# Making all gate terms of an mLSTM in the first stage of a fused attention and two-MLP kernel

## The chip, the cores and the metric

One core of a Trainium2 chip runs the kernel. The metric is the device time of the whole program in microseconds (us). The engines are TensorE (PE, with its weight loads as PEld), VectorE (DVE), ScalarE (ACT), GpSimd (POOL) and SyncE (SP), whose queue issues every DMA of this kernel.

## The reference

Three blocks follow one another, on 2 batches, 8 heads, 768 steps and a head size of 40 (16 rows of gates, 1536 tokens, width 320).

```
# 1: mLSTM, per batch and head, over steps t
m_new  = max(f[t] + m, i[t])
f_stab = exp(f[t] + m - m_new);  i_stab = exp(i[t] - m_new);  m = m_new
C = f_stab * C + i_stab * outer(v[t], k[t]);  n = f_stab * n + i_stab * k[t]
y[t] = sigmoid(o[t]) * (C @ q[t]) / max(abs(n . q[t]), 1)
# 2: x = y (1536 x 320);  h = x @ w_in (2048);  g = piecewise quadratic of h;  x = g @ w_out
# 3: 8 experts of 1024: out = sum_e P[:, e] * (relu(x @ w1[e]) @ w2[e])
#    P: exp of x @ w_gate, normalized eight times over rows and columns
```

## The kernel before, in words

The steps are cut into 6 chunks of L = 128; a chunk of one batch is a tile, so there are 12 tiles t = 0 to 11 (chunk t // 2, batch t % 2), each of 128 tokens and 8 heads.

**Gates.** All gate rows lie in one tile `g_all` (`g_i`, `g_f`, `g_x`, `g_m`). `gate_logs(a, b)` runs the max-plus scan on DVE over columns a to b and then six elementwise steps, on DVE for chunk 0 and on POOL for later columns (L376 to L385). `gate_sums` adds up the logs inside each chunk with a scan on DVE. `store_sums` writes the sums to a DRAM tile `g_d` (four small DMAs), and `load_g(t)` reads them back, spread over 128 partitions (512 KB), as the tile G of a later tile; for tile 0 and 1 `decay` makes G on PE instead. `gate_tokens` (which is `gate_by_token` and `gate_ends`) turns the sums into factors by token with small matmuls and three ACT instructions (`gt`, `nla`, `lend`). Before, chunk 0's gates are made first; chunk 1's follow inside the first stage (logs after `keys(1)`, sums after `gate_out(0)`, `gate_tokens(1, 2)` at its end); chunks 2 to 5 (four chunks, 512 columns) are made by `gates_rest(2, NCH)`, called at the end of tile 2, in the next stage.

**First stage.** Tiles 0 and 1 are written out by hand, with three pieces of the weights of block 2 between them (`pieces`; a piece is loaded raw, decoded by ACT and three DVE steps, and split in two). While `ordered[0]` is true, PE, ACT and DVE each keep the order of the text. SP's queue is in the order of the text too in this trace: `load_g(2)` stands behind `store_sums(1, 2)`.

**Next stage.** After `ordered[0] = False` the planner may reorder. Block 2's loop takes tokens 0 to 511 first, in halves of 256 (`STAGES[0]`): for two tiles of `ff` at tokens 0 to 255 (tiles 0 and 1), with six steps of the generator `attn_rest` after each, then tokens 256 to 511, for which tiles 2 and 3 must be done: until then the loop only pulls steps of `attn`. A tile's `attn` runs `values`, the causal cut of G, eight `Exp` (one a head), `scores`, `gated`, `values_sum`, `update`, `gate_out`, `turn` and `tile_x`, which writes the tile's columns of XH (ACT) and XL (DVE), the inputs of block 2's first product. In `attn(3)`, `sigmoids(4, NTILE)` stands right after `values_sum`; it needs `load_o(4, NTILE)` (1280 KB), issued in `attn(2)`. From the third block on the loop is nothing but matrix products with weights prepared a step ahead.

`warm(n)` issues n matmuls on zeros, which no result uses.

Of the kernel before, what the change touches and what calls it, by code (L numbers as in the profile page):

```python
# [11 lines left out]
ACTF = mybir.ActivationFunctionType  # L12
# [3 lines left out]
B, H, S, D = 2, 8, 768, 40  # L16
# [15 lines left out]


W0 = 14
WD = 3
WA, WG = 4, 2
RATE = (3.1, 4.5, 0, 0, 0)

# [6 lines left out]
def mlstm_moe_moe_kernel(  # L45
# [103 lines left out]
    with ExitStack() as atx:  # L149
# [11 lines left out]
        def load_gates(a, b):  # L161
            for r in range(2):
                nc.sync.dma_start((g_f, g_i)[r][0:GROW, a:b], gates[1 - r, :, a:b])
            nc.sync.dma_start(g_x[96:GROW, a:b], gates[0, 96:GROW, a:b])
# [4 lines left out]
        def store_sums(c0, c1):  # L169
            for j in range(4):  # L170
                o = j // 2 * 8 + j % 2
                nc.sync.dma_start(g_d[j * 4 : j * 4 + 4, (c0 - 1) * L : (c1 - 1) * L], g_x[o : o + 7 : 2, c0 * L : c1 * L])

        def gate_tokens(c0, c1):
            gate_by_token(c0, c1)
            gate_ends(c0, c1)

        def gates_rest(c0, c1):
            gate_logs(c0 * L, c1 * L)
            gate_sums(c0, c1)  # L180
            store_sums(c0, c1)
            gate_tokens(c0, c1)

        def tile_g(t):
            if t in (1, 3):
                return wide[:, t - 1 + t // 3, :].rearrange("p (h t) -> p h t", h=8)
# [6 lines left out]
        def load_qk(t):  # L193
            for r in range(2):
                nc.sync.dma_start(
                    QK[t % 2][r * 64 : r * 64 + 40, 0 : 2 + r : 1 + r], qk[t, r].rearrange("p (a b c) -> p a b c", a=2, b=4)
                )

        def load_kv(t):
            b = ap.tile([128, 648], F32, name="kv_t", tag="kv_t", bufs=2)  # L200
            nc.sync.dma_start(b, kvo[t][:, 0:648])
            return QK[t % 2], b, tile_g(t)

        def load_o(t0, t1):
            nc.sync.dma_start(sig[:, t0:t1, :], kvo[t0:t1, :, 648:968].rearrange("t p d -> p t d"))
# [105 lines left out]
        def load_piece():  # L311
            if len(raws) < len(M1SEQ):
                raws.append(m1_load(*M1SEQ[len(raws)]))

        load_qk(0)
        load_piece()
        load_qk(1)
        load_gates(L, 2 * L)
        tiles_in[0] = load_kv(0)
        tiles_in[1] = load_kv(1)  # L320
        load_piece()
        load_o(0, 2)
        load_piece()
        load_o(2, 4)
        load_piece()

        def m1_weights():
# [40 lines left out]
        def gate_logs(a, b):  # L368

            sl, nx = slice(a, b), slice(a + 1, b + 1)  # L370
            vec.tensor_tensor_scan(
                out=g_m[0:GROW, nx], data0=g_f[0:GROW, sl], data1=g_i[0:GROW, sl], initial=g_m[0:GROW, a : a + 1],
                op0=ALU.add, op1=ALU.max,
            )
            eng = gp if a else vec
            eng.tensor_tensor(out=g_x[0:96, sl], in0=g_f[0:96, sl], in1=g_m[0:96, sl], op=ALU.add)  # L376
            eng.tensor_tensor(out=g_x[0:GROW, sl], in0=g_x[0:GROW, sl], in1=g_m[0:GROW, nx], op=ALU.subtract)  # L377
            q = g_f[0:LROW, sl]
            eng.tensor_scalar(out=q, in0=g_x[0:LROW, sl], scalar1=CLAMP, scalar2=ROUND, op0=ALU.max, op1=ALU.add)  # L379
            eng.tensor_scalar(out=q, in0=q, scalar1=ROUND, scalar2=None, op0=ALU.subtract)  # L380
            q = g_f[64:LROW, sl]
            x = g_x[64:LROW, sl]
            if a:
                gp.tensor_scalar(out=x, in0=x, scalar1=CLAMP, scalar2=None, op0=ALU.max)  # L384
                gp.tensor_tensor(out=q, in0=x, in1=q, op=ALU.subtract)  # L385
            else:
                vec.scalar_tensor_tensor(out=q, in0=x, scalar=CLAMP, in1=q, op0=ALU.max, op1=ALU.subtract)

        def gate_sums(c0, c1):

            for c in range(c0, c1):
                cs = slice(c * L, (c + 1) * L)
                vec.tensor_tensor_scan(
                    out=g_x[0:LROW, cs], data0=ones[0:LROW, :], data1=g_f[0:LROW, cs], initial=0.0, op0=ALU.mult, op1=ALU.add,
                )
            if c0 == 0:
                act(out=gl, in_=g_x[0:48, 0:L], func=ACTF.Copy)
                vec.tensor_tensor(out=gl[32:48], in0=g_x[32:48, 0:L], in1=f(gl[32:48]), op=ALU.subtract)
# [43 lines left out]
        def scores(t, hf, tag):  # L442
            p = bank(tag)
            a = tiles_in[t][0]
            for i in range(4):
                mm(p[:, i * 128 : (i + 1) * 128], a[0:104, 1 + hf, i, :], a[0:104, 0, i, :], start=True, stop=True)
            return p
# [87 lines left out]
        def attn(t):  # L535
            c, b = divmod(t, 2)
            last = c == NCH - 1
            qk_t, _, G = tiles_in[t]
            vw = values(t)
            gp.affine_select(  # L540
                out=G, in_=G, pattern=[[0, 8], [1, 128]], compare_op=ALU.is_ge, fill=FAR, base=0, channel_multiplier=-1,
            )
            for j in range(8):
                h = b * 8 + j % 4 * 2 + j // 4
                act(out=G[:, j, :], in_=G[:, j, :], func=ACTF.Exp, bias=nla[:, c, h : h + 1])
            yield
            if t == 2:
                load_o(4, NTILE)
            A = []
            for hf in range(2):  # L550
                p = scores(t, hf, "at")
                yield
                A.append(gated(t, hf, p))
                yield
            kw = None if last else keys(t)
            pi = bank("ax")
            for pr in range(4):
                mm(pi[:, pr * 82 : (pr + 1) * 82], qk_t[0:104, 0, pr, :], Cst[:, b, pr, :], start=True, stop=True)
            pa = values_sum(A, vw, "at", WA if t < 5 else 0)
            if t == 3:  # L560
                sigmoids(4, NTILE)
            yield
            if not last:
                pu = update(kw, vw, "at")
                gp.tensor_tensor(
                    out=Cst[:, b, :, :], in0=Cst[:, b, :, :],
                    in1=lend[:, c * 8 + b * 4 : c * 8 + b * 4 + 4].unsqueeze(2).to_broadcast([104, 4, 82]), op=ALU.mult,
                )
            hv = ap.tile([128, 8, 41], F32, name="hv", tag="hv")
            vec.tensor_tensor(  # L570
                out=hv, in0=heads(pi), in1=gt[:, c, b * 8 : b * 8 + 8].unsqueeze(2).to_broadcast([128, 8, 41]), op=ALU.mult,
            )
            vec.tensor_tensor(out=hv, in0=hv, in1=heads(pa), op=ALU.add)
            sg = gate_out(t, hv)
            yield
            if not last:
                add_update(t, pu)
            px = turn(sg, "ax")
            yield
            tile_x(t, px)  # L580
            if t == 2:
                gates_rest(2, NCH)
            if t + 2 < NTILE:
                load_tile(t + 2)
            yield
# [16 lines left out]

        gate_logs(0, L)
        gate_sums(0, 1)
        vw, kw, A, pa, pu, px, sg = ({} for _ in range(7))
        pieces = [m1_piece(*M1SEQ[n], raws[n]) for n in range(3)]
        ps_ = {}
# [7 lines left out]
        A[0] = [gated(0, hf, ps_[0, hf]) for hf in range(2)]  # L615
        kw[0] = keys(0)
        next(pieces[0], None)
        decay(1, 0, "g1")
        decay(1, 1, "g1")
        vw[1] = values(1)  # L620
        for hf in range(2):
            ps_[1, hf] = scores(1, hf, "g2")
        A[1] = [gated(1, hf, ps_[1, hf]) for hf in range(2)]
        kw[1] = keys(1)
        gate_logs(L, 2 * L)
        pa[0] = values_sum(A[0], vw[0], "at", 0)
        next(pieces[1])
        sigmoids(0, 2)
        pa[1] = values_sum(A[1], vw[1], "g2", 0)
        pu[0] = update(kw[0], vw[0], "at")  # L630
        sg[0] = gate_out(0, heads(pa[0]))
        gate_sums(1, 2)
        next(pieces[1], None)
        px[0] = turn(sg[0], "ax")
        add_update(0, pu[0])
        store_sums(1, 2)
        load_qk(2)
        tiles_in[2] = load_kv(2)
        load_g(2)
        sg[1] = gate_out(1, heads(pa[1]))  # L640
        pu[1] = update(kw[1], vw[1], "g2")
        next(pieces[2])
        tile_x(0, px[0])
        warm(WD, wbank)
        px[1] = turn(sg[1], "g2")
        add_update(1, pu[1])
        sigmoids(2, 4)
        tile_x(1, px[1])
        next(pieces[2], None)
        warm(WD, wbank)  # L650
        raws[0:3] = [None] * 3
        gate_tokens(1, 2)
        load_piece()
        load_tile(3)
        load_gates(2 * L, S)
        ordered[0] = False
        wjobs = m1_weights()
        w_state = [2]

# [343 lines left out]
```

## Time and profile before

| | before |
|---|---|
| three runs, us | 1003.9, 1005.05, 1005.0 (median 1005.0) |
| the profiled execution, us | 1004.18, of which its span is 1002.4 |
| PE busy | 975.7 us (97%), mean granted clock 0.981 |
| DVE, ACT, POOL busy | 443.9, 373.0, 51.6 us |
| DMA | 52.55 MB, nearly all on SP's queue |

Times in the rows are us from the start of the span. A row of a timeline gives start, length, engine, operation, the tile written and the tile read, the shapes, how many instructions are merged into it, and in brackets the idle time before it with what ended it. A busy PE is not PE at its peak: at a granted clock of 0.50 the same matmul takes about twice as long.

### The profile page before, as it was taken

How to read it: one execution, taken by the hardware profiler on the slowest of the kernel's cores; microseconds unless marked ns; L12 is line 12 of the kernel's file. 1: busy time of each engine (PE TensorE's matmuls, PEld its weight loads, DVE VectorE, ACT ScalarE, POOL GpSimd, SP SyncE). 2: the span in 40 equal slices, each digit the busy share in tenths (PEclk: the TensorE clock that was granted, in tenths of full speed). 3: DMA queues.
4: the chain of work that ended last, by engine and by line, in shares of the span. 5: the costliest groups of instructions: out<-in, count | busy, mean ns of one | idle time of the engine just before them, and what ended most of it. 6: DMA issues, size and time to landing. Idle time of an engine off the chain costs nothing.

```text
span 1002.4 us, 13461 instructions
## 1 busy us (share of the span) xinstructions
PE 975.7 (97%) x5465; PEld 866.7 (86%) x5465; DVE 443.9 (44%) x814; ACT 373.0 (37%) x705; POOL 51.6 (5%) x63
## 2 busy tenths in 40 slices
PE   9859999999999999999999999999999999999998
PEld 6748988888887899999999999999999998999997
DVE  6756686675465563422522432252243234222222
ACT  4736575888775223311411321141132113111111
POOL 4242420000000000000000000000000000000000
PEclk9868999999999999999999999999999999999999
DMA  6834640121003000200300120030021002000000
GB/s 188 252 114 130 191 139 4 53 87 58 0 17 100 1 2 29 87 1 1 116 1 1 51 66 1 1 116 1 1 71 46 1 12 77 1 1 1 27 27 27
DMA packets 44574, 52.55 MB, mean 52 GB/s; under 512 B 3536, under 2 KB 37952, under 8 KB 44512
## 3 DMA queue, kind: packets, MB, share of 16 engines
q1 hardware_dynamic: 44512, 51.69, 17.2%
q8 instruction: 43, 0.70, 0.3%
q14 instruction: 19, 0.16, 0.0%
HBM read 49.67 MB, written 2.01 MB: 52 GB/s over the span
## 4 chain that ended last, share of the span: by engine, by line
PE 93%; DVE 3%; POOL 2%; ACT 1%; issue 1%; DMA 0%; DVEq 0%; SPq 0%; POOLq 0%
PE bk_g L69 74%; PE bk_ax L69 11%; PE bk_at L69 8%; DVE sg L69 1%; DVE den L69 0%; DMA qk<-in_qk_dram 0%; POOL g_all L379 0%; DVE Cst L69 0%; ACT scr L69 0%; DVE dv L69 0%; DVE raw L69 0%; POOL g_all L384 0%; POOL g_all L380 0%; DVE A L69 0%; POOL g_all L377 0%
## 5 line engine op out<-in xcount | busy, mean ns | idle before, releaser
L69 PE MATMUL bk_g<-XH,wk 128*128 128x512 f32 (+1 forms) x1240 | 402.7, 390 | 0.6 <-ACT XH L69 0.6
L69 DVE SCALAR_TENSOR_TENSOR lo<-bk_g,hi 128x512 fp32r<-128x512 f32 x192 | 132.7, 691 | 373.1 <-ACT hi L69 372.0
L69 PE MATMUL bk_g<-XL,wk 128*128 128x512 f32 (+1 forms) x744 | 286.2, 385 | 1.1 <-DVE XL L69 1.1
L69 ACT ACTIVATE hi<-bk_g 128x512 fp32r<-128x512 f32 x192 | 115.1, 599 | 454.2 <-PE bk_g L69 453.6
L69 PEld LDWEIGHTS bk_g<-XH,wk 128*128 128x128 f32 x1240 | 233.0, 190 | 43.5 <-ACT XH L69 1.0
L69 PE MATMUL bk_g<-wf,hi 128*128 128x320 f32 x1152 | 256.1, 308 | 0.0
L69 PEld LDWEIGHTS bk_g<-wf,hi 128*128 128x128 f32 x1152 | 199.4, 188 | 12.9
L69 PE MATMUL bk_g<-wf,lo 128*128 128x320 f32 x576 | 177.3, 308 | 0.0
L69 PEld LDWEIGHTS bk_g<-XL,wk 128*128 128x128 f32 x744 | 141.6, 190 | 23.1 <-DVE XL L69 1.4
L69 PEld LDWEIGHTS bk_g<-wf,lo 128*128 128x128 f32 x576 | 108.0, 187 | 0.2 <-DVE lo L69 0.2
L69 PE MATMUL bk_ax<-wf,hi 128*128 128x320 f32 x384 | 87.1, 308 | 0.0
L69 PEld LDWEIGHTS bk_ax<-wf,hi 128*128 128x128 f32 x384 | 64.2, 187 | 0.0
L69 ACT ACTIVATE gs<-gs 128x512 f32<-128x512 f32 x96 | 60.4, 629 | 1.9
L69 PE MATMUL bk_ax<-wf,lo 128*128 128x320 f32 x192 | 58.4, 304 | 0.0
L69 DVE TENSOR_TENSOR wf<-raw,wf 128x640 fp32r<-128x640 f32 (+2 forms) x48 | 35.9, 757 | 19.5 <-ACT wf L69 19.4
L69 DVE TENSOR_TENSOR gs<-bk_g,gs 128x512 f32<-128x512 f32 x41 | 28.3, 690 | 33.1 <-ACT gs L69 33.0
L69 ACT ACTIVATE wf<-raw 128x640 fp32r<-128x640 f32 (+2 forms) x48 | 31.0, 656 | 29.8 <-DMA raw<-in_w_dram 14.7
L69 ACT ACTIVATE wk<-raw 128x512 fp32r<-128x512 f32 (+1 forms) x42 | 26.8, 638 | 35.9 <-DMA raw<-in_w_dram 21.8
L69 ACT ACTIVATE gs<-bk_g 128x512 f32<-128x512 f32 (+1 forms) x50 | 29.7, 594 | 26.5 <-PE bk_g L69 26.0
L69 DVE SCALAR_TENSOR_TENSOR acc<-bk_g,P,acc 128x320 f32<-128x320 f32 x63 | 30.8, 545 | 15.3 <-PE bk_g L69 15.3
L69 DVE TENSOR_TENSOR wk<-raw,wk 128x512 fp32r<-128x512 f32 x40 | 27.5, 689 | 20.5 <-ACT wk L69 20.3
L69 PEld LDWEIGHTS bk_ax<-wf,lo 128*128 128x128 f32 x192 | 36.0, 188 | 0.0
(186 smaller groups left out, 799.3 us busy)
## 6 DMA issues: line engine op xcount, KB each, us to landing
raw<-in_w_dram SPq DMA_DIRECT2D x32, 320.0 KB
raw<-in_w_dram SPq DMA_DIRECT2D x32, 256.0 KB
raw<-in_w_out_dram SPq DMA_DIRECT2D x8, 640.0 KB
raw<-in_w_in_dram SPq DMA_DIRECT2D x8, 512.0 KB
raw<-in_w_dram SPq DMA_DIRECT2D x64, 64.0 KB
kv_t<-in_kvo_dram SPq DMA_DIRECT2D x12, 324.0 KB
qk<-in_qk_dram SPq DMA_DIRECT2D x24, 160.0 KB
G<-g_d SPq DMA_DIRECT2D x5, 512.0 KB
```

Source lines behind the costliest of these rows:

```text
L69: r = fn(*args, **kw)
```

## The change

All gates are made in the first stage. The logs of chunk 1 move ahead of the first `values`, its sums and `gate_tokens(1, 2)` ahead of `gated(1, ...)`; the logs of chunks 2 to 5 stand between the two `gated` of tile 1, their sums and stores at the end of the first stage, and `gate_tokens(2, NCH)` in `attn(2)`, ahead of its `scores`. `gates_rest` is gone. The transfers are reissued: the gates of chunks 1 to 5 come early, the output gates of tiles 2 and 3 and the fourth piece later, and everything that tiles 2 and 3 need stands behind `load_g(2)` and `load_g(3)`, right after the stores of chunk 1's sums. `sigmoids(2, 4)` moves ahead of `tile_x(0)`. WD grows from 3 to 4, and the warm matmuls go to another bank. The eight `Exp` of a tile are kept behind the last ACT instruction of the first stage.

```diff
-WD = 3
+WD = 4
...
-        def gates_rest(c0, c1):
-            gate_logs(c0 * L, c1 * L)
-            gate_sums(c0, c1)
-            store_sums(c0, c1)
-            gate_tokens(c0, c1)
...
         load_qk(0)
+        load_gates(L, 2 * L)
         load_piece()
         load_qk(1)
-        load_gates(L, 2 * L)
         tiles_in[0] = load_kv(0)
+        load_gates(2 * L, S)
         tiles_in[1] = load_kv(1)
         load_piece()
         load_o(0, 2)
-        load_piece()
-        load_o(2, 4)
         load_piece()
...
-                act(out=G[:, j, :], in_=G[:, j, :], func=ACTF.Exp, bias=nla[:, c, h : h + 1])
+                with tc.issue_after(start_end["act"]):
+                    act(out=G[:, j, :], in_=G[:, j, :], func=ACTF.Exp, bias=nla[:, c, h : h + 1])
             yield
             if t == 2:
+                gate_tokens(2, NCH)
                 load_o(4, NTILE)
...
             tile_x(t, px)
-            if t == 2:
-                gates_rest(2, NCH)
...
         gate_logs(0, L)
         gate_sums(0, 1)
+        gate_logs(L, 2 * L)
...
         next(pieces[0], None)
+        gate_sums(1, 2)
+        store_sums(1, 2)
         decay(1, 0, "g1")
         decay(1, 1, "g1")
         vw[1] = values(1)
-        for hf in range(2):
-            ps_[1, hf] = scores(1, hf, "g2")
-        A[1] = [gated(1, hf, ps_[1, hf]) for hf in range(2)]
+        ps_[1, 0] = scores(1, 0, "g2")
+        ps_[1, 1] = scores(1, 1, "g2")
+        gate_tokens(1, 2)
+        A[1] = [gated(1, 0, ps_[1, 0])]
+        gate_logs(2 * L, S)
+        A[1].append(gated(1, 1, ps_[1, 1]))
         kw[1] = keys(1)
-        gate_logs(L, 2 * L)
+        load_g(2)
+        load_g(3)
+        load_o(2, 4)
+        load_piece()
+        load_qk(2)
+        tiles_in[2] = load_kv(2)
+        load_piece()
+        load_qk(3)
+        tiles_in[3] = load_kv(3)
         pa[0] = values_sum(A[0], vw[0], "at", 0)
         next(pieces[1])
         sigmoids(0, 2)
         pa[1] = values_sum(A[1], vw[1], "g2", 0)
         pu[0] = update(kw[0], vw[0], "at")
         sg[0] = gate_out(0, heads(pa[0]))
-        gate_sums(1, 2)
         next(pieces[1], None)
         px[0] = turn(sg[0], "ax")
-        add_update(0, pu[0])
-        store_sums(1, 2)
-        load_qk(2)
-        tiles_in[2] = load_kv(2)
-        load_g(2)
+        next(pieces[2])
+        sigmoids(2, 4)
         sg[1] = gate_out(1, heads(pa[1]))
         pu[1] = update(kw[1], vw[1], "g2")
-        next(pieces[2])
+        warm(WD, bank("g1"))
         tile_x(0, px[0])
-        warm(WD, wbank)
+        add_update(0, pu[0])
+        next(pieces[2], None)
         px[1] = turn(sg[1], "g2")
+        warm(WD, bank("g1"))
+        tile_x(1, px[1])
         add_update(1, pu[1])
-        sigmoids(2, 4)
-        tile_x(1, px[1])
-        next(pieces[2], None)
-        warm(WD, wbank)
         raws[0:3] = [None] * 3
-        gate_tokens(1, 2)
-        load_piece()
-        load_tile(3)
-        load_gates(2 * L, S)
+        gate_sums(2, NCH)
         ordered[0] = False
+        start_end = dict(newest)
+        store_sums(2, NCH)
```

## Rows read from the trace of the kernel before

**Rows 1.** The page's forty slices of the span (25.1 us each): PE's granted clock.

```profile
PEclk9868999999999999999999999999999999999999
```

**Rows 2.** Windows: stretch, length, then busy time (instructions) of PE, PEld, DVE, ACT, POOL.

```profile
38.70:53.45 14.75, 14.38 (x113) 12.70 (x112) 14.37 (x26) 10.46 (x27) 7.77 (x8) 1.00 0.78 258
...
53.45:86.20 32.75, 18.68 (x89) 17.18 (x89) 18.41 (x37) 15.18 (x27) 9.58 (x7) 0.58 0.45 122
```

**Rows 3.** Timeline of PE: first product of block 2, tile 3, the late gates.

```profile
32.51 0.78 PE L69 MATMUL bk_g<-XH,wk 128*128 128x256 f32 x1
...
53.10 0.35 PE L69 MATMUL bk_at<-vw,A 128*128 128x41 f32 x2
60.70 1.30 PE L69 MATMUL bk_g<-cst,g_all 112*128 112x48 f32 x5 [7.26 <-DVE g_all L69]
63.97 3.77 PE L69 MATMUL bk_g<-cst,g_all 112*128 112x48 f32 x15 [1.96 <-DVE g_all L69]
```

**Rows 4.** Timeline of POOL: chunk 1's six steps, G of tile 2, chunks 2 to 5.

```profile
17.40 0.55 POOL L376 TENSOR_TENSOR g_all<-g_all 96x128 f32<-96x128 f32 x1 [1.74 <-DVE g_all L69]
...
21.18 0.45 POOL L385 TENSOR_TENSOR g_all<-g_all 16x128 f32<-16x128 f32 x1
...
32.40 1.09 POOL L540 TENSOR_SCALAR_AFFINE_SELECT G<-G 128x1024 f32<-128x1024 f32 x1 [0.50 <-DMA G<-g_d]
...
50.06 1.28 POOL L376 TENSOR_TENSOR g_all<-g_all 96x512 f32<-96x512 f32 x1 [1.62 <-DVE g_all L69]
...
58.94 1.25 POOL L385 TENSOR_TENSOR g_all<-g_all 16x512 f32<-16x512 f32 x1
```

**Rows 5.** Timelines of DVE, PE and ACT: end of tile 3, then of tile 4.

```profile
78.62 0.56 DVE L69 TENSOR_TENSOR XL<-bk_ax,XH 128x384 fp32r<-128x384 f32 x1
...
89.36 1.65 PE L69 MATMUL bk_at<-vw,A 128*128 128x41 f32 x14
...
93.74 0.26 ACT L69 ACTIVATE sg<-sg 128x64 f32<-128x64 f32 x1 [0.27 <-DVE sg L69]
...
97.15 0.55 DVE L69 TENSOR_TENSOR XL<-bk_ax,XH 128x384 fp32r<-128x384 f32 x1
```

**Rows 6.** Timeline of ACT: end of the first stage, tile 2's Exp, late sigmoids.

```profile
20.99 0.62 ACT L69 ACTIVATE Cst<-bk_at 40x164 f32<-40x164 f32 x2
...
24.89 0.74 ACT L69 ACTIVATE sig<-sig 128x640 f32<-128x640 f32 x1
...
29.52 1.28 ACT L69 ACT_TABLE_LOAD   x1
...
40.56 1.27 ACT L69 ACTIVATE G<-G,nla 128x128 f32<-128x128 f32 x4
...
68.02 1.28 ACT L69 ACT_TABLE_LOAD   x1
...
71.67 1.28 ACT L69 ACT_TABLE_LOAD   x1
```

**Rows 7.** Timeline of SP's queue: stores of sums, G of tile 2, late output gates.

```profile
22.11 2.53 SPq L172 DMA_DIRECT2D g_d<-g_all  x4
...
26.75 0.38 SPq L191 DMA_DIRECT2D G<-g_d  x1
...
46.23 0.46 SPq L205 DMA_DIRECT2D sig<-in_kvo_dram  x1
```

**Rows 8.** Windows as in rows 2; the last three: PE's clock, DMA share, GB/s.

```profile
2.25:20.25 18.00, 17.43 (x110) 13.05 (x109) 12.61 (x28) 8.00 (x16) 7.14 (x11) 0.99 0.92 258
...
32.50:86.20 53.70, 39.26 (x238) 35.99 (x236) 33.92 (x64) 27.79 (x58) 18.35 (x15) 0.71 0.61 180
100.00:160.00 60.00, 56.99 (x445) 53.16 (x445) 44.50 (x94) 40.62 (x103) 18.34 (x21) 1.00 0.47 139
```

**Rows 9.** Timeline of DVE: one decode step of a piece at two places.

```profile
24.44 0.69 DVE L69 SCALAR_TENSOR_TENSOR dv<-raw,dv 128x512 int32<-128x512 int32 x1
...
52.01 1.11 DVE L69 SCALAR_TENSOR_TENSOR dv<-raw,dv 128x512 int32<-128x512 int32 x1
```

## The prediction, made before the changed kernel ran

> **What bounds the kernel now.** I read the forty slices first, for the stretches where PE is not at full clock: all lie in the first four slices, the first 100 us; behind them it is granted 0.9 or more throughout [rows 1]. So a change to the first stage is worth what it takes out of PE's lost time there. Next the windows: from 53.45 to 86.20 PE is busy 18.68 of 32.75 us at a mean clock of 0.58, against 14.38 of 14.75 at 1.00 in the stretch ahead of it [rows 2]. Work done at full clock is about 18.68 x 0.58 = 10.8 us, so some 22 us are lost in this one stretch. Then PE's timeline says what it waits for: tile 3's `values_sum` has issued two of its sixteen products when small gate products stand next in PE's queue and wait 7.26 us, then 1.96 us, for DVE's sums [rows 3]. POOL's timeline says why these come late: the six steps for chunks 2 to 5 run from 50.06 to 60.19 [rows 4], one behind the other (0.73 us of another step lies among them). The rest of the loss follows from it: after the wait everything PE does for tile 3 runs at the lower clock level (1.2 GHz), tile 3 ends at 79.18 with its XL [rows 5], and the loop can't go on without it.
>
> **The change, part by part.**
>
> *The late gates leave tile 3's path.* Without them `values_sum(3)` goes on at 53.45. Its last 14 products take 1.65 us at full clock, as tile 4's did [rows 5]: 55.1. In tile 4, 6.7 us passed from there (91.01) to the end of XL (97.70) [rows 5]: 61.8. One thing tile 4 did not have: `sigmoids(4, NTILE)` with two table loads holds ACT for 4.93 us (68.02 to 72.95) [rows 6]. Starting at 53.45 it ends at 58.4; tile 4's first ACT step came 2.73 us after its products [rows 5], which is 57.8 here, so it is 0.6 us late. Tile 3 ends at 62.4 in place of 79.18: **-16.8 us**. Bounds: had the planner filled the wait with nothing and the clock stayed full in what follows, a further 3 us would go (the products from 79 to 84 ran at half clock); if the output gates land late (rivals), less. I take no gain in clock: PE still idles some 5 us while tile 3 ends, and behind the wait of 7.26 us the clock was the lower one [rows 2].
>
> *The gate products themselves.* They took 1.30 + 3.77 us at half clock [rows 3], some 2.5 us at full. They now stand in tile 2's stretch, where PE is busy 14.38 of 14.75 us [rows 2], so nothing hides them: **+2.5 us** (0 if they fall in a wait, 5.1 if at half clock).
>
> *POOL and DVE in the first stage.* POOL's ten us of work for chunks 2 to 5 now start behind tile 1's scan, around 17, and end near 27 to 28; tile 2's `values` and causal cut, at 32.40 before [rows 4], are the next to need POOL, so this is covered, with some 4 us to spare. Chunk 1's six steps (17.40 to 21.63, 4.2 us [rows 4]) move to about 8.5 to 13, in front of `values(0)`, which waited for its transfer until 12 anyhow. `keys(1)` could be queued behind the long steps, until 27; only `update(1)` would wait, and the end of the stage is later than that.
>
> *Transfers and ACT.* This is the part that can lose. The first batch sheds 320 + 640 KB and gains 480 KB of gates; at 258 GB/s [rows 8] it ends near 18.4 rather than 20.25. The stores of chunk 1's sums take SP 2.53 us [rows 7]; they can now start near 14 and are down near 19.5, where `load_g(2)` was issued at 26.75 before [rows 7]. Behind it go G of tile 2, G of tile 3 and the output gates of tiles 2 and 3: 1344 KB, 5.3 us at the same rate, plus up to 2.5 us until the first lands (G of tile 2, issued at 26.75 behind two other loads, was down by 32.40 [rows 4, 7]): 24.8 to 27.3. ACT, in the order of the text, gets to `sigmoids(2, 4)` near 23 and waits for that, 2 to 4 us. Queued behind it on ACT are XH of tile 0, two Cst copies, the rest of the third piece, tile 1's copy and XH, and so PE's turn of tile 1. From `sigmoids(2, 4)` to the table load took 4.63 us before (24.89 to 29.52), and the steps that are new behind it add some 1.9 (two Cst copies are 0.62 [rows 6]): block 2's first product starts at 31.4 to 33.9, before at 32.51 [rows 3]. What is saved at this place is the tail of gate work between that table load and the product. I take **+0.5 us**; bounds -1.1 and, with the next paragraph, +4.3.
>
> DVE runs beside POOL more than before: one decode step took 0.69 us with POOL idle and 1.11 us beside POOL's long steps [rows 9]. Two such steps in each of two pieces are 1.7 us, and the lighter steps around them about as much. The Trainium skill ("GPSIMD Engine Reference", "Specifications") says that GpSimd shares its SBUF interfaces with VectorE and contends with DVE instructions that read two SBUF inputs. The trace agrees (0.69 against 1.11 us); by that rule the first stage would end up to 2.9 us later, which is the upper bound just given; I don't add it whole, since ACT, not DVE, ends the stage.
>
> *Tile 2's Exp.* They ended at 41.83, behind ACT's wait for the first product [rows 6]. G and its factors are now there ahead of the stage's end, and the planner can put them first, some 4 us earlier; PE is nearly full there, so I take **-1.0 us** (0 to -4).
>
> *Weights.* DVE does 33.92 us of work between 32.50 and 86.20 [rows 8]; less some 3 us of scans, 31 are left for about 40 us, 78%. Where DVE was at 44.50 of 60 us (74%), PE lost 3.0 of 60 [rows 8]. **+1.5 us**, from 0 to twice that rate (4).
>
> Two more warm matmuls fall in PE's wait for ACT and cost nothing; without that wait, about half a us.
>
> Sum: -16.8 + 2.5 + 0.5 - 1.0 + 1.5 = -13.3. The profiled execution took 1004.18 us (span 1002.4 and 1.8 around it), which gives 990.9; the median of the runs shown is 0.8 above it. I say **991.0 us**. With every term at its worse end (no Exp gain) the sum is -16.8 + 5.1 + 4.3 + 4 = -3.4, with all at the better end about -25.
>
> **The rivals.**
>
> *Smaller gain, a new wait in tile 3.* `load_o(4, NTILE)` was issued at 46.23 [rows 7], behind four pieces, the last of which waits for a buffer that the fifth piece frees. The fourth piece now lands nearly 10 us later, and the stores of chunks 2 to 5 stand ahead of these loads on SP. If the 1280 KB (5.1 us at 258 GB/s) are issued at 53 rather than 46, `sigmoids(4, NTILE)` starts near 59 and ends at 64, and tile 3's XH stands behind it: 6 us lost, 997. Together with a DVE that is full (4 us), 1000. Against it: the raw buffers of the first three pieces are free early.
>
> *Larger gain.* The clock holds behind tile 3 (3 us), Exp early (4), first stage shorter (1): 983.
>
> *Slower.* POOL takes chunk 1's six steps only behind tile 1's `keys`. Then the sums, which stand in DVE's and ACT's order ahead of `gated(1, ...)`, come at 21 rather than 14; stores, both G, the output gates and with them ACT's whole tail move by 7 us and tile 2's queries, behind 960 KB more, by as much: 998. It decides from a shift of 13.3 us: stores not before 27, that is if the long steps are taken first as well. Against it: the text puts chunk 1 first, and its inputs are there by 8 us.
>
> *The gate work doesn't leave the path.* If the planner puts the late sums' products ahead of tile 2 and these wait for POOL, tile 2 is late by what tile 3 was: near 1004, no change. POOL's end near 28 speaks against it.
>
> **How the numbers follow.** Forecast (986 to 995.5): 0.47. Smaller gain (to 1002): 0.26. Larger gain: 0.15. No change: 0.04; slower: 0.08. A range of 983 to 1000 leaves out about 2 in 10. A measurement of this kernel tells about 0.2%, 2 us. Faster by more: 0.88; within: 0.04; slower: 0.08.
>
> **What would show it.** Right: no PE wait on `g_all` beyond 2 us after the first stage, POOL's 512-column steps over by 28, tile 3's XL near 62, stretch 53 to 86 without the long clock dip. ACT's idle before the second sigmoid shows the price of the transfers. Wrong: a wait of over 10 us for SP's transfers ahead of tile 2 or 3, or block 2's first product later than 37.

## The result and the profile after

The changed kernel takes 995.3 us (median of 4 runs, 994.4 to 996.7) against 1004.45 us for the kernel before in the same session (4 runs, 1002.3 to 1005.05): the ratio is 0.9914, with a 95% interval of 0.9893 to 0.9935, so it is faster by 0.9%. The forecast was 991.0 us in a range of 983 to 1000. The profiled execution took 996.17 us (span 994.4, mean granted clock 0.990). On the chips of the experiments below the kernel before spread from 1003 to 1018 us, its long runs at a lower mean clock (1003.38 us at 0.982, 1018.0 at 0.969), while the changed kernel kept to 993.5 to 997.1, so the ratios there stand further from 1; why it spread was not tried.

The page's granted clock of PE in forty slices, beside [rows 1]: the third slice rises from 6 to 7, the fourth from 8 to 9.

```profile
PEclk9879999999999999999999999999999999999999
```

Windows of the changed kernel (columns as in [rows 2]): the end of the first stage, and the stretch from tile 2's end to 72 us, in which tile 3 ends.

```profile
20.25:34.57 14.32, 10.71 (x49) 8.56 (x50) 12.54 (x21) 9.21 (x18) 11.76 (x9) 0.64 0.80 230
...
53.31:72.00 18.69, 11.84 (x74) 10.80 (x76) 17.19 (x34) 10.87 (x16) 3.41 (x3) 0.74 0.83 254
```

The timeline of PE: the first product of block 2, the gate products, `values_sum(3)`, and `turn` of tile 3.

```profile
21.99 3.63 PE L69 MATMUL bk_g<-vw,scr 128*128 128x41 f32 x16 [2.61 <-POOL vw L429]
...
34.57 0.47 PE L69 MATMUL bk_g<-XH,wk 128*128 128x256 f32 x1
...
36.68 1.88 PE L69 MATMUL bk_g<-cst,g_all 112*128 112x48 f32 x16
...
56.80 1.87 PE L69 MATMUL bk_at<-vw,A 128*128 128x41 f32 x16
58.50 0.94 PE L69 MATMUL bk_at<-vw,kw 128*104 128x82 f32 x8
63.97 0.66 PE L69 MATMUL bk_ax<-cst,sg 128*128 128x128 f32 x2 [4.53 <-DVE sg L69]
66.79 0.47 PE L69 MATMUL bk_ax<-cst,sg 128*128 128x128 f32 x1 [2.17 <-ACT sg L69]
```

The reader is to see three things. No wait for `g_all` of the size of [rows 3] is left: the gate products run in 1.88 us at full clock in tile 2's stretch, and `values_sum(3)` goes through at 56.80. But tile 3 now waits elsewhere: its products end at 59.44, and PE stands idle 4.53 us for DVE's `sg`, then 2.17 us for ACT's. And block 2's first product starts at 34.57, 2.06 us later than before.

POOL's timeline says that the order of the change held: chunk 1's steps first, and those of chunks 2 to 5 over by 29.83, though `values(1)` (vw) got its turn between them only at 21.02, which is PE's 2.61 us at 21.99.

```profile
8.37 0.45 POOL L369 TENSOR_TENSOR g_all<-g_all 96x128 f32<-96x128 f32 x1 [4.97 <-DVE g_all L69]
...
11.35 0.45 POOL L378 TENSOR_TENSOR g_all<-g_all 16x128 f32<-16x128 f32 x1
...
18.63 1.26 POOL L369 TENSOR_TENSOR g_all<-g_all 96x512 f32<-96x512 f32 x1 [1.90 <-DMA g_d<-g_all]
...
21.02 0.92 POOL L429 TENSOR_TENSOR vw<-kv_t,gt 128x328 f32<-128x328 f32 x1
...
28.39 1.44 POOL L378 TENSOR_TENSOR g_all<-g_all 16x512 f32<-16x512 f32 x1
```

Timelines of DVE, then of ACT, then of SP's queue.

```profile
21.38 1.10 DVE L69 SCALAR_TENSOR_TENSOR dv<-raw,dv 128x512 int32<-128x512 int32 x1
...
30.56 1.10 DVE L69 TENSOR_TENSOR dv<-raw,wk 64x512 fp32r<-64x512 f32 x1
31.69 1.47 DVE L69 TENSOR_TENSOR wk<-raw,dv 64x512 fp32r<-64x512 f32 x1
...
60.08 0.81 DVE L69 SCALAR_TENSOR_TENSOR dv<-raw,dv 128x640 int32<-128x640 int32 x1
60.82 0.48 DVE L69 TENSOR_TENSOR hv<-hv,bk_at 128x328 f32<-128x328 f32 x1
...
67.96 0.56 DVE L69 TENSOR_TENSOR XL<-bk_ax,XH 128x384 fp32r<-128x384 f32 x1
```

```profile
26.09 0.72 ACT L69 ACTIVATE sig<-sig 128x640 f32<-128x640 f32 x1
...
31.69 1.27 ACT L69 ACTIVATE wk<-dv 64x512 fp32r<-64x512 f32 x2 [1.57 <-DVE dv L69]
32.97 0.26 ACT L69 ACTIVATE sg<-sg 128x64 f32<-128x64 f32 x1
...
62.07 0.87 ACT L69 ACTIVATE wf<-raw 128x512 fp32r<-128x512 f32 x2 [2.12 <-DVE raw L69]
62.96 1.28 ACT L69 ACT_TABLE_LOAD   x1
64.26 2.34 ACT L69 ACTIVATE sig<-sig 128x2560 f32<-128x2560 f32 x1
66.50 0.24 ACT L69 ACTIVATE sg<-sg 128x64 f32<-128x64 f32 x1
...
106.69 1.57 ACT L69 ACTIVATE G<-G,nla 128x128 f32<-128x128 f32 x5 [3.94 <-POOL G L533]
...
108.64 0.24 ACT L69 ACTIVATE sg<-sg 128x64 f32<-128x64 f32 x1
```

```profile
16.23 2.51 SPq L172 DMA_DIRECT2D g_d<-g_all  x4
19.93 0.38 SPq L199 DMA_DIRECT2D sig<-in_kvo_dram  x1
23.64 0.38 SPq L185 DMA_DIRECT2D G<-g_d  x1
...
50.60 0.46 SPq L199 DMA_DIRECT2D sig<-in_kvo_dram  x1
```

Where the 8.0 us between the two spans (1002.4 and 994.4) come from is read off five moments of the two profiled executions: block 2's first product, the end of its first 16 products, the ends of XL of tiles 2 and 3, and that of tile 9 (154.35 before, 146.34 after). The forecast's +1.5 for the weights was worked out for some 40 us from 32.50 on, so it stands with tile 3.

| stretch, us | before | after | difference | forecast |
|---|---|---|---|---|
| start to first product of block 2 | 32.51 | 34.57 | +2.06 | +0.5 |
| its first 16 products (to 36.48, to 36.84) | 3.97 | 2.27 | -1.70 | 0 |
| to XL of tile 2 (52.08, 53.31) | 15.60 | 16.47 | +0.87 | +1.5 |
| to XL of tile 3 (79.18, 68.52) | 27.10 | 15.21 | -11.89 | -15.3 |
| to XL of tile 9 | 75.17 | 77.82 | +2.65 | 0 |
| to the end | 848.05 | 848.06 | 0.0 | 0 |

The sum is -8.0 where the forecast had -13.3.

### The profile page after: what moved, and what is told of

Its sections match the earlier page's. It is cut to its first block, busy times and chain, and to the rows that moved or that the text cites. A ratio compares the mean times of both kernels' runs of the same rounds, so it can differ in the third digit from the quotient of the medians.

```text
span 994.4 us, 13460 instructions
## 1 busy us (share of the span) xinstructions
PE 971.3 (98%) x5461; PEld 862.1 (87%) x5467; DVE 449.7 (45%) x814; ACT 371.6 (37%) x705; POOL 52.8 (5%) x63
## 4 chain that ended last, share of the span: by engine, by line
PE 90%; DVE 5%; ACT 2%; DMA 2%; issue 1%; SPq 0%; POOL 0%; DVEq 0%; POOLq 0%
PE bk_g L69 73%; PE bk_ax L69 11%; PE bk_at L69 6%; DMA raw<-in_w_in_dram 1%; DVE dv L69 1%; DVE den L69 1%; DVE wf L69 1%; DVE raw L69 0%; DVE sg L69 0%; ACT gs L69 0%; DMA raw<-in_w_dram 0%; DVE wk L69 0%; DVE A L69 0%; DVE hv L69 0%; ACT dv L69 0%
## 5 line engine op out<-in xcount | busy, mean ns | idle before, releaser
L69 PEld LDWEIGHTS bk_g<-wf,hi 128*128 128x128 f32 x1152 | 199.3, 188 | 13.3 <-ACT hi L69 0.4
L69 PE MATMUL bk_g<-wf 128*128 128x256 f32 (+1 forms) x192 | 36.0, 326 | 0.3 <-DVE wf L69 0.2
```

What stands on the lines that cost most here:

```text
L69: r = fn(*args, **kw)
```

## The experiments

All kernels were compared with the kernel before on the same chip, where its medians are 1011 to 1014 us. Because of its spread I compare medians with the changed kernel's own, measured again twice (the marks).

The table has all twelve runs. "To first product", "to XL 3" (from the first product) and "to XL 9" (from there) are read from the profiled execution as above. Three profiled executions of the same changed kernel had the first product at 34.57, 35.49 and 36.10, and the five kernels 6 to 10, whose edits lie behind the first stage, at 32.56 to 34.27. So less than 3.5 us is not read from that column.

| kernel | median us | ratio to before (95%) | to first product | to XL 3 | to XL 9 |
|---|---|---|---|---|---|
| changed, second time | 994.85 | 0.982 (0.978 to 0.985) | 36.10 | 33.82 | 76.54 |
| changed, third time | 995.01 | 0.983 (0.979 to 0.987) | 35.49 | 33.87 | 77.84 |
| 1 gates late, rows early | 1008.22 | 0.998 (0.995 to 1.001) | 43.78 | 36.36 | 77.82 |
| 2 before, only gates early | 1008.0 | 0.999 (0.996 to 1.003) | 37.66 | 41.16 | 74.44 |
| 3 gates and rows late | 1005.42 | 0.994 (0.991 to 0.998) | 30.41 | 47.32 | 74.72 |
| 4 logs on DVE | 997.97 | 0.985 (0.981 to 0.988) | 37.11 | 33.95 | 77.72 |
| 5 rows behind the raw piece | 999.45 | 0.986 (0.983 to 0.990) | 37.02 | 34.28 | 77.74 |
| 6 sigmoids behind XH | 994.34 | 0.983 (0.979 to 0.988) | 33.38 | 31.59 | 77.39 |
| 7 zeros in tile 3 | 994.11 | 0.984 (0.980 to 0.988) | 33.24 | 33.80 | 77.22 |
| 8 pieces held | 991.63 | 0.980 (0.976 to 0.984) | 34.27 | 30.58 | 76.74 |
| 9 as 6 and 7 | 996.54 | 0.985 (0.981 to 0.989) | 32.56 | 31.58 | 80.44 |
| 10 as 6, 7 and 8 | 992.05 | 0.981 (0.977 to 0.984) | 33.39 | 30.67 | 78.31 |

1, 2, 6 and 7 ran on one chip, the others on another. Both marks are of the second, so 1, 2, 6 and 7 have none of their own chip.

**The marks.** The changed kernel, unaltered:

> The changed kernel itself once more, as the mark for the runs on this chip: 0.985 to 0.993 of the kernel before; first product of block 2 near 34.6, tile 3's XL near 68.

> The changed kernel once more, unaltered, as the mark for the three kernels run beside it. Expected: 994 to 997 us, block 2's third tile (XL of tile 3) ending 33.5 to 34 us after that of tile 1.

The times came in as expected, and in the third run the rest did too. In the second the ratio, 0.982, lies below the range expected, as the kernel before was slower there, and the first product came at 36.10, 1.5 us later than expected.

### Is it the gates? (1, 2, 3)

**1.** In the changed kernel the gates of chunks 2 to 5 are made at tile 2's end again; their rows are still loaded early.

```diff
-                gate_tokens(2, NCH)
                 load_o(4, NTILE)
...
             tile_x(t, px)
+            if t == 2:
+                gates_rest(2, NCH)
...
-        gate_logs(2 * L, S)
...
-        gate_sums(2, NCH)
...
-        store_sums(2, NCH)
```

> The changed kernel with one part undone: the gates of chunks 2 to 5 are made at the end of tile 2 again; chunk 1's early gates, the new order of transfers and the early Exp stay. Theory G (the gain is the wait for the late gates, taken out of tile 3): PE waits 5 us or more on the sums again, tile 3's XL ends within 3 us of the kernel before's 79.18, and the time is 1002 to 1009, no better than before. Theory T (the gain comes from transfers and Exp being earlier): most of the gain stays, tile 3's XL ends before 73, time below 999.

It was not the undoing that was meant. With their rows in place the planner took the gates into the first stage by itself, and put the sums into DVE's queue where they had to wait. DVE's and PE's timelines of this kernel:

```profile
29.50 0.42 DVE L69 TENSOR_TENSOR_SCAN g_all<-ones,g_all 80x128 f32<-80x128 f32 x1 [7.00 <-POOL g_all L384]
...
34.10 0.90 PE L69 MATMUL bk_ax<-cst,sg 128*128 128x128 f32 x3 [7.01 <-DVE sg L69]
```

DVE stands still for 7.00 us ahead of a sum, with tile 0's `sg` queued behind it, and PE waits 7.01 us for that; block 2 starts at 43.78, 7.7 us or more later than in any execution of the changed kernel. The time is the one that theory G gave, but for another reason. So what is worth having is not early gates alone: the sums must stand where they wait for nothing, as the change has them, written at the stage's end.

**3.** The same, with the rows loaded late too (`load_gates(2 * L, S)` at the end of the stage):

```diff
-        load_gates(2 * L, S)
...
         raws[0:3] = [None] * 3
+        load_gates(2 * L, S)
```

> Mends the run on late gates, where the planner had pulled the late gates into the first stage by itself because their rows were loaded early. Here these rows too are loaded late, as before the change; chunk 1's early gates, the order of the other transfers and the early Exp stay. Theory G (the gain is the wait for the late gates in tile 3): TensorE waits 5 us or more on the late sums in tile 3 again and tile 3's XL ends at 76 to 84; time 1000 to 1008, against the changed kernel's 995. It can keep a few us, since GpSimd is then idle in the first stage and the first product comes 1 to 4 us earlier than in the changed kernel. Theory T (transfers and Exp): XL of tile 3 before 73, time below 999.

Now the old wait is back in PE's timeline, in three parts, and 1005.42 us stands against 994.85 for the changed kernel of the same chip, 10.6 us (7.7 between the two profiled spans, 1002.4 and 994.7):

```profile
52.81 0.31 PE L69 MATMUL bk_at<-vw,A 128*128 128x41 f32 x2
58.27 1.30 PE L69 MATMUL bk_g<-cst,g_all 112*128 112x48 f32 x5 [5.16 <-DVE g_all L69]
61.33 1.30 PE L69 MATMUL bk_g<-cst,g_all 112*128 112x48 f32 x5 [1.75 <-DVE g_all L69]
63.72 2.53 PE L69 MATMUL bk_g<-cst,g_all 112*128 112x48 f32 x10 [1.09 <-DVE g_all L69]
```

The table's row says more: from the first product to tile 3's end it takes 47.32 us instead of 33.82, that is 13.5 us, but the first product comes at 30.41, and at 32.56 to 36.10 in the eight executions with early gates. So the early gates pay 13.5 us and cost the first stage 2 to 6 us. Whether the rest of the change (chunk 1 first, the transfers, the warm products) by itself makes the first stage shorter than before (30.41 against 32.51) can't be told from one execution of each.

**2.** The other direction: the kernel before with only the gates of chunks 2 to 5 made early, nothing else moved.

```diff
         tiles_in[0] = load_kv(0)
+        load_gates(2 * L, S)
...
         gate_logs(L, 2 * L)
+        gate_logs(2 * L, S)
...
-        load_gates(2 * L, S)
+        gate_sums(2, NCH)
         ordered[0] = False
+        store_sums(2, NCH)
```

(and `gate_tokens(2, NCH)` in `attn(2)`, as in the change).

> The kernel before with one part of the change alone: the gate rows of chunks 2 to 5 are loaded early, their logs follow chunk 1's on GpSimd, their sums stand at the end of the first stage and gate_tokens(2, NCH) ahead of tile 2's scores; all else as before. Theory G: the whole gain or more, since the first stage is not made longer by anything else: tile 3's XL ends at 62 to 68, time 988 to 996. Theory T: less than half of the gain, time over 1000.

A miss for theory G: the ratio is 0.999, and the time is what theory T gave. But the wait for the gates is gone here too: the sixteen gate products run at 41.44 without one. What it gives is small, since PE now waits in tile 3 for weight steps (2.48 us for ACT at 64.47) and for `sg` (3.88 us for DVE at 76.50): tile 3 gains 5.5 us, and the first product is 5.15 us later. DVE's timeline shows two decode steps beside POOL's closely packed queue, three times as long as the 0.69 us of [rows 9]:

```profile
19.61 2.17 DVE L69 SCALAR_TENSOR_TENSOR dv<-raw,dv 128x512 int32<-128x512 int32 x1
21.82 2.25 DVE L69 SCALAR_TENSOR_TENSOR raw<-raw,dv 128x512 int32<-128x512 int32 x1
```

Here chunk 1's and the late chunks' steps follow one another on POOL from 17.73 to 34.48, and chunk 1's sums come at 26.98. That moving chunk 1 out of the way first is what lets the change keep its gain is likely, and was not tried by itself.

### What the first stage pays (4, 5)

**4.** All elementwise gate steps on DVE, POOL freed of them:

```diff
-            eng = gp if a else vec
+            eng = vec
```

(and the same choice for the one step that was written out for POOL).

> The changed kernel with the elementwise steps of gate_logs on VectorE for all chunks, none on GpSimd. It costs VectorE some 1.7 us where it idles 3.17 us (chunk 1) and some 3.5 us behind tile 1's scan (chunks 2 to 5). Theory P (the first stage is longer because GpSimd's long steps slow VectorE beside them, 1.10 us in place of 0.69, and hold tile 1's values back): the decode steps of the second and third pieces take 0.69 us again, TensorE's wait of 2.6 us for tile 1's values goes, first product of block 2 at 31 to 33, time falls by 1.5 to 3 us. Rival (the first stage waits for the raw pieces and for VectorE's own work): first product at 34 or later, time unchanged or 1 to 2 us longer.

The mechanism is there, the gain is not. The decode steps are back at 0.69 us and PE no longer waits for `vw`, but the gate steps themselves now take DVE from 19.00 to 23.72, ahead of the piece; DVE's and PE's timelines:

```profile
19.00 1.65 DVE L69 TENSOR_TENSOR_SCAN g_all<-g_all 112x512 f32<-112x512 f32 x1
...
24.82 0.69 DVE L69 SCALAR_TENSOR_TENSOR dv<-raw,dv 128x512 int32<-128x512 int32 x1
...
37.11 0.47 PE L69 MATMUL bk_g<-XH,wk 128*128 128x256 f32 x1
```

997.97 us, 3 us more than the mark. The rival holds: DVE was busy 12.54 of the changed kernel's last 14.32 us of the stage, and what is spared beside POOL is spent on the steps.

**5.** The rows of chunks 2 to 5 loaded behind the second raw piece, so that the piece isn't late (ACT had waited 2.15 us for it, to 19.94):

```diff
-        load_gates(2 * L, S)
         tiles_in[1] = load_kv(1)
         load_piece()
+        load_gates(2 * L, S)
```

> The changed kernel with the gate rows of chunks 2 to 5 loaded behind the second raw piece, not ahead of it. ScalarE waited for that piece until 19.94 (14.68 before the change). Theory R (the 480 KB ahead of it delay the first stage): the piece's first step starts by 18, the first product of block 2 comes 1 to 2 us earlier, time falls by 1 to 2 us. Rival (GpSimd beside VectorE, and values of tile 1, set the stage): less than 0.7 us.

The piece's first ACT step now comes at 17.77 without a wait, but DVE, in the order of the text, stands at the scan for the rows, and the stage ends no earlier:

```profile
18.80 1.29 DVE L69 TENSOR_TENSOR_SCAN g_all<-g_all 112x512 f32<-112x512 f32 x1 [1.36 <-DMA g_all<-in_gates_dram]
```

A miss as well, 4.6 us slower than the mark (997.0 to 1001.5 against 993.5 to 996.5). So the first stage's price is not one wait that can be taken out alone.

### What is left in tile 3 (6 to 10)

**6.** `sigmoids(4, NTILE)` behind tile 3's XH on ACT.

```diff
-            if t == 3:
-                sigmoids(4, NTILE)
...
             tile_x(t, px)
+            if t == 3:
+                with tc.issue_after(newest["act"]):
+                    sigmoids(4, NTILE)
```

> The changed kernel with the last sigmoids (tiles 4 to 11) queued behind tile 3's XH on ScalarE. In the changed kernel ScalarE holds tile 3's copy of sg for 2.65 us with them. Theory A (that wait is on the path): tile 3's XL ends 2.5 to 3 us earlier, near 65.5, and the time falls by 2 to 3 us, to 992.5 to 993.5. Rival (VectorE, which is full from 53 to 68, sets the end, or the sigmoids then delay block 2's first activations by as much): less than 1 us.

**7.** Twenty products of zeros ahead of tile 3's `turn`.

```diff
-        def turn(sg, tag):
+        def turn(sg, tag, n=0):
             px = bank(tag)
+            warm(n, px)
```

> The changed kernel with 20 matmuls on zeros in the hole that TensorE has while tile 3 ends (from its update to its turn). The stretch after the hole runs at half clock until 72.5. Theory C (the low clock behind the hole costs time): granted clock 1.00 from 64 to 74, products of block 2 there take half as long, time falls by 2 to 3 us, to 992.5 to 993.5. Rival (the work behind the hole waits for other engines anyway): clock as said, but less than 1 us.

In 6 tile 3 ends 2.3 us sooner behind the first product (31.59 for 33.9); in 7 it doesn't, though the clock does change: from 62 to 64 it is 1.00 (0.61 in the changed kernel), and the lower level holds for some 3 us there, from 66 to about 69, where the changed kernel has it from 64 to past 72. Neither moves the time by more than the spread, 994.34 and 994.11 us, as the two rivals have it, as far as marks of another chip can tell.

**8.** Block 2's loop draws no weight piece ahead of need until tile 3 is done. (Pieces that its next products need are still drawn, so DVE is not free of them.)

```diff
-                            else:
+                            elif len(done) == 4:
                                 pump_w()
```

> The two weight pieces that VectorE prepares during tiles 2 and 3 of the changed kernel are held back until tile 3 is done. Theory W (what is left of tile 3's tail is VectorE's queue, full with the pieces between 53 and 68 us): the add behind tile 3's last product starts within 0.5 us of it, the sigmoid table's load no longer ends after it, and tile 3 ends 31.5 to 32 us after tile 1 instead of 33.7; whether the kernel keeps that depends on what the pieces push back behind tile 3: 992 to 995 against the mark's 995. Rival (ScalarE's order holds the tail, the pieces only fill time that is free): tile 3 ends 33 to 34 us after tile 1, and the time is the mark's or up to 3 us more, since the pieces now stand beside tiles 4 and 5.

Theory W holds, and by more than it asked: 991.63 us (989.6 to 993.5) against 995.01 (994.0 to 997.1) for the mark of the same chip, 3.4 us less, and the two sets of runs don't overlap. It is the fastest version of this study. Timelines of SP's queue, DVE, ACT and PE of this kernel:

```profile
42.61 1.48 SPq L199 DMA_DIRECT2D sig<-in_kvo_dram  x1
...
58.90 0.48 DVE L69 TENSOR_TENSOR hv<-hv,bk_at 128x328 f32<-128x328 f32 x1
...
60.94 0.44 DVE L69 TENSOR_SCALAR dv<-dv 128x640 int32<-128x640 int32 x1
...
64.29 0.56 DVE L69 TENSOR_TENSOR XL<-bk_ax,XH 128x384 fp32r<-128x384 f32 x1
...
59.11 1.28 ACT L69 ACT_TABLE_LOAD   x1
60.41 2.34 ACT L69 ACTIVATE sig<-sig 128x2560 f32<-128x2560 f32 x1
62.65 0.24 ACT L69 ACTIVATE sg<-sg 128x64 f32<-128x64 f32 x1
...
61.93 0.66 PE L69 MATMUL bk_ax<-cst,sg 128*128 128x128 f32 x2 [2.80 <-DVE sg L69]
62.94 0.47 PE L69 MATMUL bk_ax<-cst,sg 128*128 128x128 f32 x1 [0.35 <-ACT sg L69]
```

The `hv` add starts at 58.90 and not at 60.82, and the piece whose steps stood ahead of it (59.08, 60.08) now starts at 60.94. ACT's table load for the sigmoids starts earlier too, at 59.11 and not at 62.96: in the changed kernel two weight steps on ACT stand ahead of it that wait 2.12 us for DVE (62.07). So PE waits 2.80 + 0.35 us in place of 4.53 + 2.17. What the pieces push back is not seen behind tile 3: from there to tile 9 it takes 76.74 us, and 76.54 to 77.84 in the changed kernel.

The edit moves more than DVE's work, though. A piece that is not drawn issues no load either, so the output gates of the later tiles go out at 42.61 and not at 50.60, and the queries of tile 4 at 50.32 and not at 59.62. In the changed kernel the transfers ahead of the sigmoids were over at about 57.1 (DMA share 1.07 from 56 to 57, 0.07 from 57 to 58), 5.9 us before the table load, so it did not wait for them. But that the 3.4 us come from DVE's queue alone, and none from the earlier loads, is not shown.

**9, 10.** The edits of 6 and 7 together, without and with held pieces.

> The two edits that each shortened tile 3 or its successor a little, together: the sigmoids of block 2's later tiles behind tile 3's normalisation on ScalarE, and 20 products of zeros in tile 3's idle stretch of TensorE (they add nothing to the result). If the hole in tile 3 and the half clock behind it are two separate costs: 2 to 3 us below the mark. If the stretch from tile 5 to tile 7 gives back what is won (tile 6's wait for GpSimd's cut and ScalarE's queue): less than 1 us below the mark, with tile 4 ending 2 to 4 us earlier and tile 7 ending within 1 us of the mark's.

> The same two edits with the held weight pieces: the version with the shortest tail of tile 3 that the three parts allow. If the three costs are separate: 3 to 5 us below the mark, tile 3 ending 30 to 31 us after tile 1. If ScalarE and VectorE were each other's cover in that tail: no more than the version without the held pieces, within 1 us.

Neither adds up: 996.54 and 992.05 us, against 995.01 and 991.63 without the two edits, so 9 is no faster than the mark, and what 10 has is 8's. Tile 3 does end early (31.58 and 30.67), and PE is at full clock through it, but the time to tile 9 grows by 2.6 and 1.6 us. Windows of kernel 10 (columns as in [rows 2] and [rows 8]) and its PE's timeline show where:

```profile
70.00:72.00 2.00, 0.65 (x6) 0.44 (x4) 0.46 (x1) 1.99 (x6) 0.44 (x1) 1.00 0.43 124
72.00:74.00 2.00, 1.08 (x6) 0.75 (x7) 1.48 (x3) 2.00 (x7) 0.68 (x1) 0.97 0.06 19
74.00:76.00 2.00, 2.00 (x11) 2.00 (x11) 0.50 (x1) 2.00 (x6) 1.10 (x2) 0.50 0.44 93
...
58.10 4.52 PE L69 MATMUL bk_ax<-wz 128*128 128x512 bf16 x19
...
72.86 1.04 PE L69 MATMUL bk_at<-wz 128*128 128x512 bf16 x3 [2.22 <-DVE A L69]
```

PE, faster now, comes 2.22 us too early to tile 4's `values_sum`, which needs the eight `Exp` that ACT starts at 70.74, behind the sigmoids and a table load. In 70 to 74 PE is busy 1.73 of 4 us, and from 74 to 80 the clock is at its lower level. The full clock was won in one place and lost in the next.

## Why the prediction was right, and where it was off

The mechanism was the one forecast, and the time lies in the range, 4.3 us above the figure. Between the two spans the sum is 5.3 us off; 1.70 us that nobody had forecast (warm products, below) are in it, without which it would be 7 us off, so that much is luck. Of the signs named, PE's wait on `g_all` is gone and POOL is done near 28 (29.83); but tile 3's XL ends at 68.52 and not near 62, and the clock dip is shorter and not gone (0.50 from 64 to 72). Step by step:

**The late gates leave tile 3's path.** Right in kind, and shown by 3: with late gates the waits and 13.5 us come back. The term was mis-sized: -16.8 forecast, -11.9 measured. Two parts make up the 4.9 us. `values_sum(3)` starts 3.5 us behind XL of tile 2, and 1.0 before (53.10 [rows 3], 52.08), as PE first takes products of block 2; that is 2.5 us. And from its start to tile 3's end it takes 11.72 us, where the forecast had 9.3 (53.10 to 62.4) from tile 4 [rows 5]; that is 2.4 us. The forecast saw one of the causes, ACT's sigmoids, at 0.6 us late; they were 2.7 late (the `sg` copy came at 66.50, with its input ready at 63.8), since ACT had stood 2.12 us at a weight step in front of them (62.07).

**Weights.** This term, +1.5 with bounds of 0 and 4, was where the other cause stood, and it was taken too low. Kernel 8 puts it at 3.4 us, with the transfers that move along. The forecast made it from a share of busy time over 40 us; but DVE was full just where tile 3's chain passed through it, 17.19 of 18.69 us from 53.31 to 72.00, and the chain's steps on DVE stood between those of the pieces: `values_sum(3)` ended at 58.67, and the `hv` add that reads it started at 60.82, 2.15 us later (0.55 in kernel 8).

**The gate products.** +2.5 forecast; the first sixteen took 1.88 us and the last four, at 43.51, 0.42: 2.3 us, at full clock and without cover, as said.

**First stage.** +0.5 forecast, +2.06 measured, by another way than the one written down. As the eight executions of this stage differ by 3.5 us, the size refutes nothing; the way does. SP did not keep the order of the text: the output gates were issued at 19.93, ahead of both G (23.64), so the second `sigmoids` (26.09) waited for nothing, and the 2 to 4 us of ACT's wait did not come. What came was DVE, which the forecast left aside ("ACT, not DVE, ends the stage"): ACT's step at 31.69 waits 1.57 us for DVE, and tile 1's `sg` and XH stand behind it. In the other seven executions that wait is 0.24 to 0.49, but DVE is full in all: from its first step on the second piece (20.64 here, 18.27 to 22.16 in the others) to its last on the third it waits 0.8 us or less, and block 2's first product follows 13.9 to 14.4 us behind that first step. So the executions differ by what lies ahead of it.

GpSimd's neighbourhood is a part of it. The two decode steps took 1.10 and 1.11 us beside POOL, and 0.69 in kernel 4, where POOL had no gate work. The same stretch, from DVE's first step on the second piece to the first product, is 12.74 us long in kernel 4 and 12.19 in kernel 3, whose POOL had no late gates either: 1.2 to 2.2 us less. The Trainium skill ("GPSIMD Engine Reference", "Specifications") has the contention for DVE instructions that read two SBUF inputs; the rows agree with it where steps are longer, and the 2.9 us that were bounded by it were not too little (its parts, 1.7 us and "about as much", would make 3.4). Not every step beside POOL is longer: in the kernel before two decode steps, at 53.79 and 54.39, took 0.68 us, the first wholly beside a POOL step of 2.25 us that started at 52.66. That the contention alone set the 2 to 6 us is not shown: kernel 4 took it away and paid as much for the steps themselves.

**Warm products.** Forecast as free and worth nothing. Block 2's first sixteen products took 2.27 us for 3.97, as the clock was at its upper level from the first on (before, it was 0.50 until about 36.5). It was at 1.00 from 32 to 33 already, ahead of the six products of zeros (33.45 to 34.92): from 21.99 to 31.63 PE had run with one gap of 0.22 us, where before it had stood still for 2.65 us ahead of 29.86. What the zeros add was not tried by itself.

**Tile 2's Exp.** Forecast -1.0 with +2.5 for the products: +1.5 for the stretch, +0.87 measured. The Exp ended 8.4 us behind the first product (42.98), and 9.3 before (41.83).

**Later tiles.** 2.65 us are lost between tile 3 and tile 9, and one place has more than that: tile 8's `Exp` wait 3.94 us for POOL's cut (106.69) with tile 6's `sg` copy (108.64) queued behind them on ACT. From XL of tile 5 to that of tile 6 it takes 11.9 us, and 8.7 before. In kernel 8, where the copy stands ahead of the `Exp`, it is 9.5. It is an order the planner chose, and it was not in the forecast.

Of the rivals, the smaller gain (997 to 1000) had the right place, tile 3's tail, and nearly the right reason: `load_o(4, NTILE)` was issued at 50.60, 4.4 us later than before [rows 7], yet they were in by about 57.1, and it was the table load at 62.96, behind weight steps, that was late. The slower case did not come about: POOL took chunk 1 at 8.37, and the stores went out at 16.23.

## What to carry to other kernels

When a stall is taken out of a chain, price what follows by the queues that the chain passes through at that place, instruction by instruction, and not by the engines' mean load: here background work for weights stood in the queue of the tail's engine, and one line that drew it later (and moved its transfers) returned 3.4 us beside a gain of 9. Work moved into an earlier stage must be fed and queued where it waits for nothing; the same gates moved alone gained nothing. A moment read from one profile is worth what other profiles of the same stage leave of it: here they differ by 3.5 us. A clock kept high by filler is worth only as much as the next wait leaves of it.

## What the runs showed of the hardware

A decode step on DVE (128x512, two inputs) took 0.69 us with POOL idle [rows 9]; beside POOL's steps it took 0.68 (53.79 in the kernel before), 1.10 (21.38 in the changed kernel), and 2.17 and 2.25 (kernel 2): the lengthening is not one factor.

A wait of PE does not always bring the lower level of its clock. In kernel 8 a wait of 1.16 us ahead of 74.02 left it at 1.00; in kernel 10 the 2.22 us ahead of 72.86 were followed by 0.50.
